# Range sums on ScalarE, merged small products and a new order list in a two-branch sequence kernel

## Chip, core and metric

The kernel runs on one core of a Trainium2 chip. The metric is the device time of one execution in microseconds (us). TensorE is called PE, VectorE DVE, ScalarE ACT, GpSimd POOL; SP is the engine that issues most DMA transfers.

## The reference

Two branches read the same x (2048 rows, 512 columns, bf16) and are mixed by a gate per row:

```python
g = _sigmoid((x * gate_w).sum(-1, keepdims=True))
a = _A_ref(x, ...)      # h[t] = Lam_bar * h[t-1] + B_bar x[t];  y = 2 Re(C h) + x * Dskip
b = _B_ref(x, ...)      # 32 heads of 16: q, k, v; features softmax(+-q w_phi), softmax(+-k w_phi)
                        # o = phi_q (phi_k^T v) / (phi_q . sum phi_k + 1e-6);  b = o @ wo
return g * a + (1 - g) * b
```

Branch a is a diagonal complex recurrence over 2048 steps with 512 states. Branch b is attention without a softmax over rows: the keys and values are first summed into a 32 x 16 matrix per head, and then every query reads that sum.

## The kernel before, in words

The fast path is one program of about 790 tasks (matmul groups, evacuations of PSUM, vector steps, DMA issues). `_fast_path` describes the tasks, and the tuple `ORDER` near the top of the file gives the sequence in which they are written out and, for each, the engine out of those that it may run on. Nothing is decided on the chip: each engine works through its own list in order, and waits in it for its operands. `pl.at(...)` and the costs in the tasks feed only the choice of buffers.

The rows of x are dealt out in four phases (f, rows 4r + f) of 512 rows. Phase 0 is loaded straight and transposed on PE (L435), in four blocks; phases 1 to 3 come by DMA transpose. Six warm-up matmuls on a zeroed tile `warm` (L425) come before, and one more after each of the first two blocks (L437). DVE writes that tile (L309). Then follow, interleaved:

- v_unit (L453): the values of 128 rows, evacuated by ACT into `vx`.
- parameters (L508 to L567): the recurrence's 512 coefficients on DVE, in tiles of 128 x 16, a complex product as four real ones.
- diagonal blocks (L583 to L589): for eight groups of states a 128 x 128 block `dgL`, the sum of the identity scaled by one column and of `swap` (the identity with halves exchanged) scaled by another. Each scaling is an instruction on ACT or DVE.
- block matrix BD (L643 to L650): w_phi without its mean, put on a block diagonal; fold (L660) multiplies it into the query and key weights.
- g_unit (L680, L685): the input of the recurrence for one group of states, carried through the four phases by a product with `dgL`. The last phase goes by DMA (L694) into a layout for the scan; scan_unit (L718 to L736) rotates, scans and rotates back on DVE; `Zs` takes the states by DMA (L748); fill_unit (L760 to L768) makes the states of the other three phases.
- k_unit (L792 to L823): keys of 256 rows, exp of plus and minus them on ACT into `E`, four sums by halves on DVE (L809) down to the softmax denominators `st1`, Ln and Exp for the reciprocal on ACT, the scaling (L816), and the sum over rows into two PSUM banks. A maximum over the denominators goes into `smax` (L812).
- q_unit (L880): the same for the queries, transposed.
- nums and smalls (L962 to L1025): numerators and denominators per head; a maximum over the query denominators goes into `qmax` (L1010).
- mix (L1027 to L1079): for each 128 rows, two scalings (L1039, one for plus and one for minus), their sum (L1041), a DMA transpose (L1056), the y products (L1048, L1052) and the product with Wo (L1065) into the same bank, the gate (L1072 or L1074), and the store (L1078).
- flag (L1101 to L1116): the gate's largest argument and the two kinds of maxima are compared with limits; if one is over, a general path runs afterwards. The flag is turned on PE, reduced, and loaded by every engine.

Of the kernel before, what the change touches and what calls it, by code (L numbers as in the profile page):

```python
# [18 lines left out]
P = 128  # L19
# [103 lines left out]
def kernel(  # L123
# [49 lines left out]
    8, 4, 6, 10, 12, 156, 14, 16, 158, 18, 22, 174, 0, 25, 176, 20, 192, 2, 162, 160, 26, 178, 196, 28, 32, 34,  # L173
    268, 30, 166, 200, 194, 36, 198, 760, 38, 276, 40, 132, 42, 164, 134, 180, 202, 44, 138, 46, 85, 73, 764, 270,
    762, 278, 77, 55, 184, 136, 272, 140, 274, 504, 168, 508, 74, 380, 506, 83, 766, 61, 182, 170, 186, 142, 79,
    208, 70, 382, 172, 81, 154, 510, 296, 298, 288, 86, 768, 144, 284, 146, 287, 212, 292, 148, 294, 96, 59, 512,
    95, 291, 56, 514, 150, 518, 211, 517, 306, 300, 67, 152, 332, 308, 302, 48, 770, 310, 304, 50, 520, 524, 523,
    65, 526, 528, 536, 338, 63, 53, 334, 446, 312, 314, 336, 342, 68, 316, 340, 772, 448, 318, 538, 322, 530, 532,
    534, 450, 344, 324, 440, 215, 444, 478, 472, 544, 320, 540, 546, 346, 326, 328, 442, 348, 330, 350, 452, 354,
    454, 456, 356, 548, 458, 474, 358, 480, 462, 460, 464, 482, 476, 216, 466, 218, 570, 98, 628, 360, 542, 384,  # L180
    100, 222, 484, 224, 362, 88, 630, 486, 226, 564, 102, 550, 104, 220, 552, 234, 602, 228, 108, 106, 488, 554,
    568, 236, 574, 566, 490, 112, 572, 230, 468, 110, 232, 494, 188, 556, 116, 248, 388, 238, 390, 250, 240, 242,
    114, 576, 190, 470, 372, 496, 252, 386, 352, 596, 578, 558, 580, 244, 606, 394, 392, 118, 254, 582, 400, 492,
    498, 586, 604, 588, 396, 600, 374, 598, 120, 694, 364, 402, 398, 500, 590, 404, 560, 608, 376, 124, 246, 406,
    256, 412, 688, 378, 408, 610, 414, 258, 612, 502, 562, 366, 122, 410, 690, 128, 692, 696, 260, 614, 416, 262,
    636, 638, 368, 632, 126, 720, 420, 698, 640, 370, 700, 422, 726, 592, 424, 618, 800, 634, 418, 616, 594, 702,
    620, 90, 642, 622, 788, 802, 728, 426, 648, 730, 722, 264, 724, 704, 644, 792, 650, 654, 646, 93, 652, 428,
    732, 790, 660, 656, 706, 734, 708, 710, 658, 662, 736, 668, 664, 670, 672, 430, 204, 812, 738, 742, 712, 206,
    280, 130, 432, 666, 818, 804, 782, 624, 776, 744, 714, 674, 794, 434, 816, 282, 814, 746, 626, 822, 820, 784,
    786, 716, 718, 748, 778, 750, 796, 780, 676, 806, 798, 810, 808, 436, 678, 758, 824, 756, 754, 752, 830, 1020,  # L190
    978, 996, 266, 984, 828, 850, 826, 854, 832, 848, 980, 852, 1302, 1314, 1022, 680, 856, 983, 986, 682, 858,
    1320, 860, 834, 998, 989, 438, 864, 684, 866, 1026, 1038, 1025, 836, 1316, 868, 1318, 1040, 1001, 862, 870,
    990, 1008, 872, 1010, 1306, 1304, 918, 842, 992, 1013, 886, 1028, 1043, 906, 882, 995, 1031, 1128, 878, 884,
    888, 912, 874, 1086, 1110, 902, 686, 1088, 876, 880, 908, 1308, 1090, 904, 898, 838, 1068, 1092, 1310, 900,
    1112, 1312, 1070, 890, 894, 930, 1130, 840, 1002, 1122, 892, 1094, 896, 1124, 846, 1072, 1004, 1014, 1044,
    1006, 914, 844, 920, 1032, 1104, 1096, 1046, 1098, 1074, 1106, 1034, 1126, 1016, 1076, 1048, 1018, 1036, 910,
    1050, 1052, 916, 1100, 1324, 1078, 1108, 924, 1200, 936, 1080, 1082, 1054, 1322, 1290, 1132, 926, 1202, 1058,
    1164, 1060, 1134, 1254, 1136, 1152, 1114, 922, 938, 928, 1138, 1204, 1116, 1158, 1154, 1062, 1166, 932, 1064,
    1084, 1066, 1188, 942, 1268, 1284, 1236, 1118, 1248, 1286, 1206, 1160, 1292, 1168, 1208, 1120, 1156, 1266,
    1190, 1182, 1176, 1184, 1288, 1232, 1102, 1193, 1210, 1162, 1270, 1256, 1170, 1194, 1186, 1178, 1230, 1294,  # L200
    1146, 1250, 1172, 1196, 1198, 1238, 1174, 1140, 948, 1234, 1276, 1056, 1142, 1148, 1272, 944, 1274, 1344,
    1180, 1150, 1144, 1212, 1214, 1252, 940, 1346, 946, 1332, 1216, 954, 1296, 1240, 1278, 1362, 1220, 1258, 1348,
    1334, 934, 1242, 1298, 1222, 1326, 1224, 950, 1380, 1226, 1364, 952, 1336, 1244, 1476, 1228, 1436, 1260, 1328,
    1368, 1366, 1434, 1452, 1440, 1280, 1370, 1262, 1438, 1356, 1382, 1350, 1442, 1372, 1392, 1454, 1352, 1478,
    1394, 1330, 956, 1338, 1358, 1354, 1396, 1458, 1386, 1416, 1340, 960, 1300, 1444, 1470, 1282, 1456, 1388,
    1374, 1418, 1360, 1376, 1472, 962, 1420, 1462, 972, 1460, 1390, 1384, 1378, 958, 1474, 1342, 974, 1398, 1426,
    1400, 1446, 1422, 1464, 1402, 966, 1480, 1448, 1424, 1406, 1265, 964, 1466, 1408, 1410, 1428, 1468, 1450,
    1412, 968, 1494, 1414, 1512, 1506, 1508, 1510, 970, 976, 1482, 1430, 1526, 1524, 1516, 1484, 1432, 1530, 1514,
    1247, 1528, 1496, 1488, 1534, 584, 1518, 1490, 740, 1492, 1542, 1544, 1546, 1532, 1520, 1548, 1498, 1536,
    1218, 1404, 774, 1487, 1500, 1523, 1552, 1550, 1538, 1502, 1554, 1566, 1557, 1505, 1560, 1541, 1568, 1570,  # L210
    1562, 1558, 1564)
# [18 lines left out]
def _fast_path(ctx, tc, A_x, A_Lambda_re, A_Lambda_im, A_B_re, A_B_im, A_C_re, A_C_im, A_log_dt, A_Dskip,  # L230
# [20 lines left out]
    warm = ctile([P, D], BF16, "warm")  # L251
# [16 lines left out]
    dgS = ctile([P, NT, P], BF16, "dgS")  # L268
# [16 lines left out]
    smax = ctile([P, NTI // 2], F32, "smax")  # L285
    qmax = ctile([P, NG], F32, "qmax")
    fl = ctile([P, 4], F32, "fl")
# [21 lines left out]
    nc.vector.memset(warm[:], 0.0)  # L309
# [42 lines left out]
    pl = _Plan({"DVE": 2.4e3, "ACT": 4.4e3, "PE": 1.1e3, "SP": 27.0e3})  # L352
# [34 lines left out]
    d_x = [pl.at(t) for t in (3.7, 4.5, 6.4, 8.4, 9.8, 11.5, 19.5)]  # L387
    d_wv0, d_wv, d_b, d_wk, d_wq, d_wo = (pl.at(t) for t in (4.5, 5.5, 17.0, 22.7, 24.8, 27.0))
    d_vec, d_wc = pl.at(9.5), pl.at(20.5)
# [5 lines left out]
    d_set = pl.at(6.2)  # L395
# [7 lines left out]
    def s_swap(e):  # L403
        for h in range(2):
            nc.vector.tensor_copy(out=swap[:, h * 64:h * 64 + 64], in_=ident[:, 64 - h * 64:128 - h * 64])
# [17 lines left out]
    def warm_fn(e):  # L423
        for _ in range(NWARM):
            MM(out=bw.t[:], lhsT=warm[:, 0:P], rhs=warm[:], start=True, stop=True)  # L425
# [4 lines left out]
    for a in range(4):  # L430
        b = pl.buf(*A1)

        def tr(e, b=b, a=a):
            for kt in range(KT):
                nc.tensor.transpose(bfv(b)[:, kt * P:(kt + 1) * P], xn[:, a, kt * P:(kt + 1) * P], ident[:])  # L435
            if a < 2:
                MM(out=bw.t[:, 0:256], lhsT=warm[:, 0:P], rhs=warm[:, 0:256], start=True, stop=True)  # L437
# [28 lines left out]
    def col():  # L466
        return sp[:, next(k_), :]
# [1269 lines left out]
```

## Time and profile before

| | us |
|---|---|
| median of 10 runs | 149.97 (149.59 to 151.3) |
| the profiled execution | 149.56 |
| its span, first to last instruction | 147.8 |
| PE busy | 140.6 |
| DVE busy | 129.4 |
| ACT busy | 115.2 |
| scalings of the mix, L1039 (32 of 128 x 512) | 12.1 |
| maxima over k sums, L812 (8 of 128 x 128) | 2.2 |
| fp32 product of 128 x 1024 on DVE, L629, each | 1.22 |

The profile holds one execution. A group of instructions is shown by its line, its engine, what it writes and reads, how often, and its busy time with the mean of one. Neighbouring instructions on one engine overlap by some 80 ns in these durations, so the distance between two starts is a little shorter than the mean duration. A wait is put down to what came last. Because durations and waits come from one execution, a sum made from them is set against that execution's own 149.56 us.

### The profile page before, as it was taken

The page shows a single profiled execution, that of the slowest core. Times are in us where ns is not written, and L with a number is a line of the kernel's source. Part 1 is how long each engine was busy: PE and PEld are TensorE (multiplying, and loading weights), DVE is VectorE, ACT ScalarE, POOL GpSimd, SP SyncE. Part 2 cuts the span into 40 slices and gives each one's busy share as a digit, 9 for nine tenths or more (in the row PEclk, how much of TensorE's full clock was granted, in tenths as well). Part 3 has the DMA queues.
Part 4 walks back from the last instruction along what each step waited for, and adds up shares of the span by engine and source line. Part 5 has one row for each costly group of instructions (what it writes and reads, how often), then busy time and mean ns, then how long its engine had stood idle before and what let it go on. Part 6 is the DMA issues. An engine that isn't in the chain of part 4 may idle for free.

```text
span 147.8 us, 3009 instructions
## 1 busy us (share of the span) xinstructions
PE 140.6 (95%) x1012; PEld 81.3 (55%) x1030; DVE 129.4 (88%) x378; ACT 115.2 (78%) x261; POOL 5.5 (4%) x15
## 2 busy tenths in 40 slices
PE   6899999999999999999999989999999999999990
PEld 2545567555665666556546545565556556445550
DVE  2328998998999999997999999999999999999610
ACT  3449899988889999889899889998787986751140
POOL 8600000000000000000000000000000000000000
PEclk9999999999999999999999999999999999999999
DMA  4999999930200031315993222143043713534712
GB/s 115 275 240 236 165 172 234 211 75 0 53 18 0 4 71 36 101 41 130 143 140 108 95 71 91 56 72 74 0 142 72 75 35 85 111 88 120 160 58 70
DMA packets 37307, 14.94 MB, mean 101 GB/s; under 512 B 29480, under 2 KB 37288, under 8 KB 37288
## 3 DMA queue, kind: packets, MB, share of 16 engines
q1 hardware_dynamic: 35824, 13.59, 44.0%
q10 hardware_dynamic: 1304, 1.12, 2.4%
q8 instruction: 9, 0.15, 0.4%
q14 instruction: 10, 0.08, 0.2%
q0 software_dynamic: 160, 0.01, 0.1%
HBM read 1.60 MB, written 2.10 MB: 25 GB/s over the span
## 4 chain that ended last, share of the span: by engine, by line
PE 83%; DVE 7%; DMA 5%; issue 1%; ACT 1%; SPq 0%; DVEq 0%
PE pp L680 19%; PE pp L1048 17%; PE pp L792 9%; PE pp L453 9%; PE pp L1065 8%; PE pp L962 5%; PE pp L685 4%; PE pp L880 3%; DMA late<-late 2%; DMA c<-c 2%; PE pp L1052 2%; PE pp L425 2%; PE pp L823 2%; DVE c L728 2%; PE pp L660 1%
## 5 line engine op out<-in xcount | busy, mean ns | idle before, releaser
L680 PE MATMUL pp<-xT,BT 128*128 128x512 bf16 x123 | 31.5, 381 | 0.2
L1048 PE MATMUL pp<-CT,Gs 128*128 128x512 bf16 (+1 forms) x99 | 23.5, 362 | 0.2
L680 PEld LDWEIGHTS <-BT 128*128 128x128 bf16 x128 | 17.8, 145 | 8.8
L1072 ACT ACTIVATE late<-pp,Gg 128x512 bf16<-128x512 f32 (+1 forms) x16 | 10.8, 673 | 11.1 <-PE pp L1065 10.9
L243 ACT ACTIVATE ET<-pp 128x512 bf16<-128x512 f32 x32 | 17.7, 612 | 1.0 <-PE pp L880 1.0
L243 ACT ACTIVATE E<-pp 128x512 bf16<-128x512 f32 x32 | 17.7, 607 | 0.2 <-PE pp L792 0.2
L1065 PE MATMUL pp<-Wo,late 128*128 128x512 bf16 (+1 forms) x67 | 16.1, 367 | 0.2 <-DMA late<-late 0.2
L453 PE MATMUL pp<-Wv,xT 128*128 128x512 bf16 x61 | 15.6, 386 | 0.6 <-ACT xT L381 0.5
L792 PE MATMUL pp<-Wk,xT 128*128 128x512 bf16 x64 | 15.6, 380 | 0.0
L880 PE MATMUL pp<-xT,Wq 128*128 128x512 bf16 x61 | 15.1, 379 | 0.5 <-DVE elate L978 0.3
L1048 PEld LDWEIGHTS <-Gs 128*128 128x128 bf16 x104 | 9.7, 98 | 7.9
L381 ACT CAST Gs<-pp 128x512 bf16<-128x512 f32 x20 | 11.7, 593 | 2.3 <-PE pp L685 2.3
L962 PE MATMUL pp<-KS,ET 128*128 128x144 bf16 (+1 forms) x128 | 12.0, 225 | 0.1
L970 ACT CAST late<-pp 128x384 bf16<-128x384 f32 (+1 forms) x24 | 10.3, 455 | 2.0 <-PE pp L962 2.0
L962 PEld LDWEIGHTS <-ET 128*128 128x128 bf16 x128 | 9.2, 98 | 4.3 <-issue 0.8
L970 ACT CAST elate<-pp 128x512 bf16<-128x512 f32 (+2 forms) x20 | 9.6, 513 | 2.0 <-PE pp L962 1.9
L816 DVE TENSOR_TENSOR E<-E,rc 128x2048 bf16<-128x2048 bf16 x8 | 9.7, 1218 | 0.5 <-ACT rc L243 0.5
L792 PEld LDWEIGHTS <-xT 128*128 128x128 bf16 x64 | 6.1, 98 | 6.9
L381 ACT CAST vx<-pp 128x512 bf16<-128x512 f32 x16 | 9.0, 588 | 0.7 <-PE pp L453 0.7
L453 PEld LDWEIGHTS <-xT 128*128 128x128 bf16 x64 | 5.8, 98 | 6.5 <-ACT xT L381 0.8
L880 PEld LDWEIGHTS <-Wq 128*128 128x128 bf16 x64 | 5.9, 97 | 6.3 <-issue 0.4
L728 DVE TENSOR_TENSOR_SCAN c<-sp,c 128x512 bf16<-128x512 f32 x8 | 9.3, 1208 | 0.0
(180 smaller groups left out, 252.4 us busy)
## 6 DMA issues: line engine op xcount, KB each, us to landing
Zs<-c SPq DMA_DIRECT2D x32, 64.0 KB, 2.1
out_dram<-late SPq DMA_DIRECT2D x9, 128.0 KB, 1.9
c<-c SPq DMA_DIRECT2D x16, 64.0 KB, 2.0
CT<-ET SPq DMA_DIRECT2D x8, 128.0 KB, 5.6
out_dram<-late ACTq DMA_DIRECT2D x6, 128.0 KB, 2.2
Wo<-in_B_wo_dram SPq DMA_DIRECT2D x4, 128.0 KB, 3.0
xn<-in_A_x_dram SPq DMA_DIRECT2D x2, 128.0 KB, 3.4
Wv<-in_B_wqkv_dram ACTq DMA_DIRECT2D x1, 256.0 KB, 3.4
```

What stands on the lines that cost most here:

```text
L243: return nc.scalar.activation(**kw)
L381: nc.scalar.copy(out=o, in_=view(b))
L453: MM(out=f32v(b), lhsT=xT[:, kt, tcols(f, a)], rhs=Wv[:, kt, :], start=(kt == 0), stop=(kt == KT - 1))
L680: MM(out=f32v(b), lhsT=BT[:, kt].rearrange("p r (q t) -> p (r q) t", t=NT)[:, :, j + 4 * h], rhs=xT[:, kt, f * NCH:(f + 1) * NCH], start=( ...
L728: nc.vector.tensor_tensor_scan(out=bw_.t[:, ri], data0=rb, data1=b1.t[:, ri], initial=0.0, op0=ALU.mult, op1=ALU.add)
L792: MM(out=f32v(b), lhsT=xT[:, kt, tcols(f, a)], rhs=Wk2[:, kt, :], start=(kt == 0), stop=(kt == KT - 1))
L880: MM(out=f32v(b), lhsT=Wq2[:, kt, g * P:(g + 1) * P], rhs=xT[:, kt, f * NCH:(f + 1) * NCH], start=(kt == 0), stop=(kt == KT - 1))
L962: MM(out=f32v(b)[:, i * w:(i + 1) * w], lhsT=ets[f].t[:, q // HG, q % HG, cs], rhs=KS[:, q // HG, q % HG, 0:w], start=True, stop=True)
L970: nc.scalar.copy(out=o2.t.rearrange("p a b -> p (a b)")[:, q0 * P:(q0 + n) * P].rearrange("p (q c) -> p q c", c=P), in_=blk()[:, :, 0:P])
L1048: MM(out=f32v(py)[:, 0:w], lhsT=st, rhs=CT[:, tt // 2 + 4 * (tt % 2), n * w:n * w + w], start=(tt == 0), stop=False)
L1065: MM(out=f32v(py)[:, 0:w], lhsT=oT.t[:, g, :], rhs=Wo[:, g, hs], start=False, stop=(g == HG - 1))
L1072: nc.scalar.mul(out=ot.t[:, hs], in_=f32v(py)[:, 0:w], mul=Gg[:, ti:ti + 1])
```

## The change

- The warm-up matmuls read a constant tile of ones that every program sets up at its start on POOL. The memset on DVE is gone. After the first block of x there is one more warm-up matmul, of 512 columns.
- The four diagonal blocks of a half are one DVE product: a pattern with ones on both diagonals (`swap` now holds the identity plus its exchanged halves), times a table `dgW` of fp32 weights that is set by four small copies. The separate scalings are gone.
- The parameter products are made two at a time on tiles of 128 x 32 (`p5`, `p6`).
- BD is made with one masked product for all four blocks, after a fused subtraction of the mean.
- The k denominators of all pairs are kept in one tile `Sk`. In place of the maxima, ACT sums them along the row with its accumulator, once over all 1024 (k) and once per phase over 256 (q), into columns of `fl`. Each sum is compared with the limit; the flag is the smallest of the comparisons.
- The two scalings of a tile in the mix are one instruction over 1024 elements.
- `ORDER` is a new list, with new costs and due times.

```diff
-    warm = ctile([P, D], BF16, "warm")
+    warm = nc.const_aps.tensor(1.0, [P, D], BF16)
...
-    nc.vector.memset(warm[:], 0.0)
...
-            nc.vector.tensor_copy(out=swap[:, h * 64:h * 64 + 64], in_=ident[:, 64 - h * 64:128 - h * 64])
+            VT(out=swap[:, h * 64:h * 64 + 64], in0=ident[:, 64 - h * 64:128 - h * 64], in1=ident[:, h * 64:h * 64 + 64], op=ALU.add)
...
-            if a < 2:
-                MM(out=bw.t[:, 0:256], lhsT=warm[:, 0:P], rhs=warm[:, 0:256], start=True, stop=True)
+            for w in ((512, 256), (256,), (), ())[a]:
+                MM(out=bw.t[:, 0:w], lhsT=warm[:, 0:P], rhs=warm[:, 0:w], start=True, stop=True)
...
-            VT(out=t2, in0=pwr[n - 1], in1=lr_, op=ALU.mult)
-            VT(out=t3, in0=pwi[n - 1], in1=li_, op=ALU.mult)
-            VT(out=t4, in0=pwr[n - 1], in1=li_, op=ALU.mult)
-            VT(out=t5, in0=pwi[n - 1], in1=lr_, op=ALU.mult)
+            VT(out=tX, in0=pw[n - 1], in1=two(lr_), op=ALU.mult)
+            VT(out=tY, in0=pw[n - 1], in1=two(li_), op=ALU.mult)
...
+    def w_dl(e):
+        for v, hs in ((lr_, ((0, 0), (64, 1))), (ns1, ((0, 1), (64, 0)))):
+            for p0, half in hs:
+                nc.vector.tensor_copy(out=dgW[p0:p0 + 64, :, half].rearrange("p (j h) -> p j h", h=2),
+                                      in_=v[p0:p0 + 64, 8:16].rearrange("p (h j) -> p j h", h=2))
+    t_wdl = pl.add({"DVE": 330.0}, w_dl, deps=[tp4], rank=6)
...
-            parts.append(pl.add({"ACT": 330.0, "DVE": 165.0}, scaled(dgL[:, tt, :], ident[:], lr_[:, ucol(tt)]), deps=[tp3], rank=6 - jj))
-            parts.append(pl.add({"ACT": 330.0, "DVE": 165.0}, scaled(dgS[:, tt, :], swap[:], ns1[:, ucol(tt)]), deps=[tp4, t_swap], rank=6 - jj))
...
+            VT(out=dgL[:, s_].rearrange("p t (h c) -> p t h c", h=2), in0=swap[:].rearrange("p (h c) -> p h c", h=2).unsqueeze(1).to_broadcast([P, 4, 2, 64]),
+               in1=dgW[:, s_].unsqueeze(3).to_broadcast([P, 4, 2, 64]), op=ALU.mult)
...
-        t_sx.append(pl.add(_dve(128), lambda e: nc.vector.tensor_reduce(
-            out=smax[:, pair:pair + 1], in_=b1.t[:].rearrange("p a b c -> p (a b c)"), axis=AX.X, op=ALU.max), deps=prev, bufs=[b1], rank=-3))
...
+    dump = iot[:].bitcast(BF16)
+    t_fk = pl.add({"ACT": 1060.0}, lambda e: aact(out=dump, in_=Sk[:].rearrange("p a b c -> p (a b c)"), func=ACT.Copy, accum_out=fl[:, 1:2]),
+                  deps=t_sx + t_tab)
...
-        t_qm.append(pl.add(_dve(256), lambda e: nc.vector.tensor_reduce(out=qmax[:, f:f + 1], in_=smv()[:, :, 0, :], axis=AX.XY, op=ALU.max),
-                           deps=[x3], bufs=[b], rank=r_))
+        t_qm.append(pl.add({"ACT": 430.0}, lambda e: aact(out=dump[:, 0:256].rearrange("p (a b) -> p a b", b=8), in_=smv()[:, :, 0, :], func=ACT.Copy,
+                                                          accum_out=fl[:, 2 + f:3 + f]), deps=[x2, t_fk], bufs=[b], rank=r_))
...
-        for sgn in range(2):
-            def sc(e, sgn=sgn):
-                v = o2.t[:, sgn].rearrange("p (g d h) -> p g d h", g=HG, d=Dh)
-                VT(out=v, in0=v, in1=als[f].t[:, a, sgn * H:(sgn + 1) * H].rearrange("p (g h) -> p g h", g=HG).unsqueeze(2).to_broadcast([P, HG, Dh, 8]), op=ALU.mult)
+        def sc(e):
+            v = o2.t.rearrange("p s (g d h) -> p (s g) d h", g=HG, d=Dh)
+            VT(out=v, in0=v, in1=als[f].t[:, a].rearrange("p (g h) -> p g h", h=8).unsqueeze(2).to_broadcast([P, 2 * HG, Dh, 8]), op=ALU.mult)
```

In the instruction lists that result, PE has the same matmuls plus the one of 512 columns, DVE 337 compute instructions in place of 379, and ACT 259 in place of 270 (DMA issues counted). DVE takes over from ACT two evacuations of G, one of x, two final ones and six small copies. The order of the loads at the start is unchanged. On PE the second block's transposes and warm-up now come before the first V product. The ACT sum over k stands between the last two evacuations of G. Among the last Wo products no two stand next to each other, as one pair did before.

## The prediction

> **What bounds the kernel now.** I read four views: the busy line of the page, the table of stretches, the chain of work that ended last, and the waits. First the busy line and four of the ten-microsecond stretches.
>
> ```profile
> PE 140.6 (95%) x1012; PEld 81.3 (55%) x1030; DVE 129.4 (88%) x378; ACT 115.2 (78%) x261; POOL 5.5 (4%) x15
> ```
>
> ```profile
> 0.00:10.00 10.00, 8.26 (x47) 3.84 (x47) 2.85 (x22) 4.12 (x6) 5.46 (x15) 1.00 0.84 208
> ...
> 50.00:60.00 10.00, 9.89 (x69) 6.16 (x69) 10.00 (x21) 9.51 (x20) 0.00 (x0) 1.00 0.19 48
> ...
> 80.00:90.00 10.00, 9.48 (x112) 5.81 (x111) 9.93 (x31) 8.77 (x21) 0.00 (x0) 1.00 0.26 85
> ...
> 140.00:147.80 7.80, 3.73 (x28) 2.26 (x26) 0.90 (x3) 1.85 (x3) 0.00 (x0) 1.00 0.26 71
> ```
>
> In a stretch the first two numbers after its length are PE and PEld, then DVE and ACT. A busy PE need not be a PE at its peak, so I checked it: the chain shows four 128x512 matmuls in 0.86 us again and again, 0.216 us each. Costing the whole instruction list at the pace of the chain (512 columns 0.216, 144 columns 0.062, 128 columns 0.056, 68 columns 0.032, one column 0.024) gives 138.3 us. The first pieces run at half that pace (0.457 us for 512 columns), which adds 2.3. The sum, 140.6, is the busy time: **PE is the bound, and it streams without gaps almost throughout.** DVE is as full (10.00 of 10 in six stretches) but PE hardly ever waits for it. What can be won is PE's idle time, 147.8 - 140.6 = 7.2 us: 1.74 in the first stretch, 0.5 spread over 10 to 80, 0.52 in 80 to 90, 0.35 in 90 to 140, and 4.07 in the last. Of the last, 3.88 lies behind PE's last matmul (143.92): the flag's way through DVE, its load and the branch. The change leaves that part as it is.
>
> The two ends of the chain and PE's named waits:
>
> ```profile
> 0.95 0.28 DVE warm L309
> 1.28 2.74 PE pp L425 x6
> 4.02 0.44 PE pp L435 x4
> 4.48 0.59 ACT xT L381
> 5.12 0.93 PE pp L453 x2
> 6.05 0.23 PE pp L435 x4
> ...
> 136.89 0.32 PE pp L1065 x2
> 137.21 3.51 DMA late<-late
> 140.76 1.04 PE pp L1065 x4
> ```
>
> ```profile
> PE pp L425 <- DVE warm L309: 1.3, 1, 1.3
> ...
> PE pp L453 <- ACT xT L381: 0.5, 1, 0.5
> ...
> PE pp L880 <- DVE elate L978: 0.3, 1, 0.3
> ...
> PE pp L1065 <- DMA late<-late: 0.2, 1, 0.2
> ```
>
> So PE begins at 1.28 because DVE's memset of the warm-up tile comes first; it stands idle 0.46 us before the first V product, for ACT's copy of the first transposed block; it waits 0.3 us for a DVE copy that frees a PSUM bank; and near the end about 0.35 us for a DMA transpose (four matmuls from 139.55 end at 140.41, the next starts at 140.76). The chain's 3.51 us of DMA there is not idle PE: other products run under it.
>
> **The change, part by part.** *Constant warm-up.* The memset (0.27 us) and PE's wait for it go. Nothing else of the kernel holds PE's first matmul; ACT and DVE begin at 0.83 and 0.95, so PE should begin near 0.95: 0.33 earlier. One 512-column dummy is added (0.457 at the slow pace), the second block's transposes and its dummy move ahead of the first V product, and the copy that this product waits for goes to DVE (425 ns for the same tile instead of 585). New start: six dummies 0.95 to 3.69 (the first x block was there at 3.54), transposes to 4.13, dummies to 4.82, transposes to 5.26, dummy to 5.49, then two V products, then two that need ACT's copy of the second block (0.2 + 0.585 after 5.26, so 6.05). The wait of 0.46 is filled, with dummy work in part. When the pace doubles decides the rest. In the trace the slow pace ends between 5.12 and 6.05. Counted from PE's first matmul that is up to 4.7 us, so 5.65 in the new kernel, and two V products end near 5.97, the next two follow at 6.05, and the point where 16 transposes and the first four V products are done moves from 7.26 to 6.95: -0.3. The Trainium skill (TensorE: Matmul & The Clock Gate, "What's actually happening") speaks against that: the activity window is free-running and does not begin with the kernel. If the pace then changes at the same 6.05 on the span's clock, the point is at 7.1: -0.16. The same rule allows a change as early as some 3.4 us after the start, an estimate from that page, which gives about -0.5, since the third V product then waits for the copy. The granted clock reads 1.00 in every row, so only the pace shows this. I take **-0.25**, ends -0.1 and -0.5. Next in line are the loads: the first half of x for the next block landed at 7.9 (issued 2.64, 5.3 to landing) and is needed at 8.6, B at 16.1 (10.84 and 5.3), needed at 17.9. Close, but none late.
>
> *DVE work removed.* Spacing of like instructions in the timeline, not their mean, is the price. Eight maxima over k sums (mean 280 ns, spacing near 200): -1.6. Four over q sums (two in 0.74 us, so 0.33 each): -1.3. Parameter products: 29 instructions took 3.23 us, 0.11 each; nine fewer: -1.0. Scaling: two of 418 ns took 0.75 us, so 0.67 for a pair; one of 1024 elements has a spacing of 0.60: 16 times 0.07 is -1.1. Block matrices: 13 scalings at 0.165 and two sums at 0.34 make 2.8 (and three ACT scalings of 0.42); the new way is four small copies (0.5) and two products of 128x512 with fp32 weights. bf16 rows of that size show 418 ns; the skill's page VectorE: DVE Perf Modes ("The perf-mode tier table") says that a tensor_tensor with fp32 input runs at single rate, and the fp32 row (1220 ns for 1024) gives 0.61 to 0.69 at half the size. By the bf16 row the part saves 1.5 us, by the rule 1.0; I take 1.0. BD in three instructions instead of seven: -0.4. Together about -6.4 us of DVE. The new list gives DVE work of ACT's: two more 512-column evacuations of G, one of x, two final ones and six small copies, about +3.7. DVE ends near 126.
>
> *What moves to ACT.* One sum over 1024 elements (nearest row: the table sine of that size, 1060 ns) and four over 256 (418): +2.7. Away go three diagonal scalings, the five evacuations and the small copies: -5.6. ACT ends near 112, with 2 to 3 us idle in each ten after 110. The accumulator's own price is shown by no row: between nothing and, if it needs a separate read of the size of the smallest ACT rows, 0.2 us each, +1.0 in all; I take nothing.
>
> None of this is on the path while PE streams: 9 us of savings on engines that PE doesn't wait for are worth nothing by themselves. They are worth what PE waits for late operands.
>
> *The new order.* PE gets the same matmuls plus one dummy (0.22 at full pace, under the wait). What it can take back is 0.52 in 80 to 90, 0.35 in 90 to 140, 0.35 at the DMA and perhaps 0.1 in 10 to 80. DVE is about 2 us ahead by 80 us (smax, parameters, blocks and BD lie before it), so the PSUM copy and the K-V blocks that set the waits there come sooner: -0.35 (ends 0 and -0.7). At the end the last Wo products are each separated by a group of other products in the new list, where before two stood together, so the DMA transpose has cover: -0.3 (ends 0 and -0.4). Rest: -0.1 (ends +0.3 and -0.2).
>
> **Sum.** -0.25 - 0.35 - 0.3 - 0.1 = -1.0 us. The profiled execution took 149.56 (span 147.8 and 1.76 around it), so about 148.6. The median of the ten runs is 149.97, 0.4 above it, since four of the ten lie near 150.9; the same step from the median gives **149.0**.
>
> **Rivals.** *PE bound, nothing returned but the start.* Against my sum speaks that PE's waits from 10 to 140 are many and tiny (0.05 us per stretch), which look like hand-over times that no order removes, and that a new order makes its own small waits. Then only -0.1 to -0.4 is left, and the median is 149.7. *ACT stands in the way: slower.* The 1.06 us sum over k sits in ACT's list between the two last evacuations of G for the last scan, and waits for the last k sum from DVE. Behind it wait that evacuation, its exchange by DMA (3.44 us in the chain), the scan and the second half of the y products. Those products come about 1.2 us earlier in the new list (94.5 against 95.7), and the last Z copies, estimated from the end of issue at 93.05, land near 94.6. If DVE's k sum is late, the delay is 1.06 plus that lateness; it decides once the delay is over the 1 us or so that DVE is now ahead. A delay of 2.5 us would leave PE idle for about 1.5 past the cover: 149.97 - 0.25 + 1.5 = 151.2. For it: DVE was at 10.00 of 10 there. Against it: its lead. *A large return:* the pace doubles early (-0.5) and nearly all inner waits go (-1.3): 148.2. *Not doing what it says:* the constant operand could hold PE's first matmul as long as the memset did; -0.25 becomes 0, 149.2.
>
> **How the numbers follow.** About 0.5% (0.75 us) is what a measurement of this kernel can tell from no change, so faster means below 149.2. My forecast with its own range 148.6 to 149.4: 0.50. Large return: 0.12. Start alone, or a warm-up that starts no sooner: 0.27. ACT in the way: 0.11. The likeliest gives 149.0. Down to 148.1 and up to 150.1 no more than two in ten are left out: the lower end takes the early doubling with the middle of the rest, the upper end the mild form of the ACT delay. Faster: 0.5 x 0.85 + 0.12 + 0.05 of the start alone = 0.60. Slower by over 0.75: 0.09. Same: 0.31.
>
> **What would show it.** First warm-up matmul near 0.95 and no gap before the first V product; the half-pace pieces ending by 6.0; the first B product near 17.9 to 18.1, not 18.44; the stretch 80 to 90 at 9.8 or more for PE; no PE wait for a DMA transpose near the end; PE's last matmul near 142.9 and 3.9 us behind it as before. DVE near 126 and ACT near 112 busy would confirm the costs. I am wrong if PE shows new waits for ACT or the Z copies from 85 to 100, or if PE's idle time between first and last matmul stays near 2.0 us.

## The result and the profile after

| | before | after | ratio, 95% interval |
|---|---|---|---|
| median of the runs taken together with the change | 150.59 us (51 runs) | 149.42 us (14 runs) | 0.9935 [0.9914, 0.9956] |
| the same, second series | 150.19 us (42 runs) | 149.55 us (7 runs) | 0.9939 [0.9916, 0.9961] |

The change takes 0.6% off, about 0.95 us, which is the step that the prediction made from its median (149.97 to 149.0, a ratio of 0.9935). The medians of the kernel before differ from series to series (149.94 to 150.59), so only ratios within a series are compared below. A ratio is the estimate on record and not the quotient of the two medians, which is 0.9922 in the first series and 0.9957 in the second; steps of 0.2% are not to be read from either.

The two profiles that are shown side by side do not show that gain: the profiled execution of the changed kernel took 150.02 us (span 148.1), one of the slowest of its runs, and that of the kernel before 149.56, one of its fastest. This has to be kept in mind while reading them. The busy line and five stretches of the profile after:

```profile
PE 141.4 (95%) x1013; PEld 81.5 (55%) x1031; DVE 127.9 (86%) x336; ACT 112.8 (76%) x257; POOL 5.3 (4%) x15
```

```profile
0.00:10.00 10.00, 8.40 (x40) 3.59 (x41) 2.89 (x18) 3.80 (x6) 5.27 (x15) 1.00 0.92 179
50.00:60.00 10.00, 9.95 (x60) 6.17 (x60) 10.00 (x19) 9.55 (x20) 0.00 (x0) 1.00 0.18 46
80.00:90.00 10.00, 9.89 (x122) 6.25 (x122) 9.86 (x26) 9.89 (x24) 0.00 (x0) 1.00 0.29 94
90.00:100.00 10.00, 9.61 (x84) 6.04 (x85) 9.97 (x32) 9.46 (x23) 0.00 (x0) 1.00 0.46 87
140.00:148.10 8.10, 4.34 (x38) 3.17 (x36) 1.45 (x7) 1.16 (x2) 0.00 (x0) 1.00 0.25 69
```

PE is still the bound, DVE and ACT have become a little lighter. The stretch 80 to 90 went from 9.48 to 9.89 for PE; ACT went from 8.77 to 9.89 there. The next stretch takes most of that back: it fell to 9.61 from the 9.95 of the profile before,

```profile
90.00:100.00 10.00, 9.95 (x86) 6.11 (x86) 10.00 (x34) 9.49 (x21) 0.00 (x0) 1.00 0.29 71
```

since PE's waits that were at 83.7 and 88.6 now stand at 90.3 and 91.7. The last stretch has more PE work because everything is later in this execution. Why, the waits of PE and pieces of the chain tell:

```profile
PE pp L421 <- PEq L1715: 0.9, 1, 0.9
PE pp L449 <- DMA xT<-in_A_x_dram: 0.5, 1, 0.5
PE pp L875 <- DVE elate L975: 0.2, 1, 0.2
PE pp L959 <- ACT iot L241: 0.2, 1, 0.2
```

```profile
2.64 6.69 DMA xT<-in_A_x_dram
9.38 1.90 PE pp L449 x8
...
19.00 2.59 PE pp L676 x12
...
143.32 0.87 PE pp L1060 x8
```

PE begins at 0.93 now, the wait for the memset is gone and so is the one for ACT's copy before the first V product. In their place stands a wait of 0.54 us at 9.38 for the first rows that come by DMA transpose: they landed 6.7 us after their issue, where the profile of before had 5.3 for the same issue in the same list. So the first B product (L676) came at 19.00, not at 18.44. At the other end the wait for the DMA transpose before the last Wo products is gone. L959 waits for ACT's `iot`, which is where the new q sum dumps its elements.

Two things are needed to read PE's idle time. A product of 512 columns is shown with 0.38 us though the next one starts 0.216 after it, so an idle time that the profile shows is about 0.16 us less than what the stop costs from start to start: the 0.19 us at the end of the profile before cost 0.35. And the two profiles hold 1012 and 1013 products where PE loaded weights for 18 more; in the eight profiles that hold 1030 or 1031 products most of the idle gaps of 0.05 us are absent. In each of the two profiles gaps of that size, 18 and 20 of them, make up 1.0 us of PE's idle time. The starts around such a gap are 0.43 us apart, the time of two products, so they look like products without a record rather than waits.

### The profile page after: what moved, and what is told of

It is laid out like the page before. It is cut to its first block, busy times and chain, and to the rows that moved or that the text cites. A ratio compares the mean times of both kernels' runs of the same rounds, so it can differ in the third digit from the quotient of the medians.

```text
span 148.1 us, 2969 instructions
## 1 busy us (share of the span) xinstructions
PE 141.4 (95%) x1013; PEld 81.5 (55%) x1031; DVE 127.9 (86%) x336; ACT 112.8 (76%) x257; POOL 5.3 (4%) x15
## 4 chain that ended last, share of the span: by engine, by line
PE 78%; ACT 7%; DMA 6%; SPq 5%; issue 1%; DVE 0%
PE pp L1043 19%; PE pp L676 18%; PE pp L1060 9%; PE pp L787 9%; PE pp L449 7%; DMA xT<-in_A_x_dram 5%; PE pp L959 4%; PE pp L681 3%; SPq L743 3%; PE pp L1047 2%; ACT ET L241 2%; ACT late L967 2%; PE pp L875 2%; PE pp L818 2%; DMA Zs<-c 1%
## 5 line engine op out<-in xcount | busy, mean ns | idle before, releaser
L676 PE MATMUL pp<-xT,BT 128*128 128x512 bf16 x125 | 31.7, 381 | 0.2
L676 PEld LDWEIGHTS <-BT 128*128 128x128 bf16 x128 | 17.9, 145 | 8.9 <-issue 0.3
L241 ACT ACTIVATE ET<-pp 128x512 bf16<-128x512 f32 x32 | 18.2, 618 | 0.6 <-PE pp L875 0.5
L1067 ACT ACTIVATE late<-pp,Gg 128x512 bf16<-128x512 f32 (+1 forms) x14 | 9.4, 675 | 10.8 <-PE pp L1060 10.8
L241 ACT ACTIVATE E<-pp 128x512 bf16<-128x512 f32 x32 | 17.1, 602 | 0.4 <-PE pp L787 0.3
L959 PE MATMUL pp<-KS,ET 128*128 128x144 bf16 (+1 forms) x128 | 12.4, 225 | 0.2 <-ACT iot L241 0.2
L377 ACT CAST Gs<-pp 128x512 bf16<-128x512 f32 x18 | 10.4, 593 | 2.3 <-PE pp L676 1.8
L959 PEld LDWEIGHTS <-ET 128*128 128x128 bf16 x128 | 9.3, 98 | 4.8 <-issue 0.5
L967 ACT CAST elate<-pp 128x384 bf16<-128x384 f32 (+2 forms) x21 | 9.6, 499 | 2.2 <-PE pp L959 2.2
L967 ACT CAST late<-pp 128x384 bf16<-128x384 f32 (+2 forms) x23 | 10.0, 486 | 1.3 <-PE pp L959 1.1
```

The costliest lines, as they stand in the source:

```text
L241: return nc.scalar.activation(**kw)
L377: nc.scalar.copy(out=o, in_=view(b))
L676: MM(out=f32v(b), lhsT=BT[:, kt].rearrange("p r (q t) -> p (r q) t", t=NT)[:, :, j + 4 * h], rhs=xT[:, kt, f * NCH:(f + 1) * NCH], start=( ...
L959: MM(out=f32v(b)[:, i * w:(i + 1) * w], lhsT=ets[f].t[:, q // HG, q % HG, cs], rhs=KS[:, q // HG, q % HG, 0:w], start=True, stop=True)
L967: nc.scalar.copy(out=o2.t.rearrange("p a b -> p (a b)")[:, q0 * P:(q0 + n) * P].rearrange("p (q c) -> p q c", c=P), in_=blk()[:, :, 0:P])
L1067: nc.scalar.mul(out=ot.t[:, hs], in_=f32v(py)[:, 0:w], mul=Gg[:, ti:ti + 1])
```

## The experiments

All ratios are to the kernel before, in the same series. To compare profiles whose starts differ I use four marks of each one: the time at which PE's clock was granted in full (the start of the trace's first clock record), the start of the first B product (the chain puts it some 0.16 later, since neighbours overlap), the distance from there to the end of PE's last matmul, and what lies behind that.

| kernel | ratio, 95% interval | profiled us | full clock from | first B at | to PE's last | behind it |
| --- | --- | --- | --- | --- | --- | --- |
| before, first profile |  | 149.56 | 5.81 | 18.27 | 125.65 | 3.85 |
| before, again | 1.0012 [0.9992, 1.0032] | 149.34 | 4.48 | 18.16 | 125.43 | 3.85 |
| old list, constant | 0.9977 [0.9961, 0.9992] | 150.25 | 3.69 | 19.01 | 125.59 | 3.85 |
| old list, light DVE | 0.9987 [0.9962, 1.0012] | 150.00 | 5.15 | 18.08 | 126.18 | 3.85 |
| old list, all else | 1.0025 [1.0008, 1.0043] | 149.84 | 3.56 | 17.93 | 126.27 | 3.85 |
| after | 0.9935 [0.9914, 0.9956] | 150.02 | 5.22 | 18.84 | 125.50 | 3.78 |
| after, again | 0.9939 [0.9916, 0.9961] | 149.64 | 3.80 | 17.94 | 126.13 | 3.78 |
| new list, memset | 0.9955 [0.9931, 0.9980] | 149.51 | 6.13 | 18.31 | 125.52 | 3.79 |
| new list, one dummy | 0.9934 [0.9911, 0.9957] | 149.83 | 6.67 | 18.61 | 125.54 | 3.78 |
| new list, heavy DVE | 1.0452 [1.0412, 1.0492] | 157.96 | 6.55 | 18.48 | 133.81 | 3.78 |
| new list, sums on DVE | 1.0032 [1.0016, 1.0048] | 150.39 | 4.77 | 17.91 | 126.91 | 3.78 |
| k sum late | 0.9953 [0.9936, 0.9970] | 149.04 | 4.11 | 17.95 | 125.52 | 3.78 |
| k sum late, q sum early | 0.9958 [0.9940, 0.9977] | 148.91 | 3.77 | 17.81 | 125.53 | 3.78 |
| the same, x loaded by ACT | 1.0088 [1.0055, 1.0120] | 150.46 | 5.16 | 19.38 | 125.51 | 3.78 |

My theory at the outset: the lighter engines alone are worth nothing, and the gain is in the start and in the list's cover of waits. The rivals: the relief of VectorE is the gain; and the loads, not the warm-up, decide the start.

### Both kernels once more

No edit. For the kernel before:

> The kernel before, unchanged, profiled once more. If the landing of the first loads varies from execution to execution by a microsecond (theory: load variation), this profile has other landing times than the first one (x, second group of rows: 5.3 us from issue to landing there) and the first B product moves with them, 18.4 to 19.0; the ratio is 1.000 within 0.3%. If the landings are a property of the list (rival), they are 5.3 us again and the first B product stands at 18.44 within 0.05.

For the changed kernel:

> The changed kernel, unchanged, profiled once more. Load variation: the xT rows land 5.3 to 6.7 us after their issue, and when they land at the short end PE doesn't wait at 9.4 and the first B product comes at 18.1 to 18.4 instead of 19.00, the span near 147.2. List (rival): the 0.54 us wait at 9.4 is there again with the same landing times, and the span is 148.1 within 0.1. Ratio to before 0.992 to 0.995 by both.

**Measured.** The repeat of the kernel before is at 1.0012, so differences of 0.2% are within the noise. Its xT loads landed in much the same time (median 5.3 us from issue, 5.1 in the first profile) and the first B product came 0.1 us from where it was; for this kernel the two executions don't show the variation. The changed kernel does: median landing 5.4 instead of 6.1, no wait at 9.4, the first B product at 17.94, 0.9 us earlier than in its first profile. But its span fell by only 0.3, to 147.85 and not to the 147.2 that was expected. Of the 0.9 us, 0.6 was lost again on the way to PE's last matmul (126.13 against 125.50), in a wait that the first profile had not:

```profile
PE pp L959 <- ACT ET L241: 0.4, 1, 0.4
```

It stands at 83.9, and ACT is named for it, but the last thing that PE's queue waits for there is DVE: it passes that wait at 83.81, 0.04 after DVE's last K-V block. DVE's timeline of the same execution shows where it comes from. The bracket is the idle time ahead of an instruction and what ended it:

```profile
69.79 0.69 DVE L713 TENSOR_TENSOR c<-c,Tcs 128x1024 bf16<-128x1024 bf16 x1 [0.52 <-DMA c<-c]
...
83.62 0.16 DVE L860 TENSOR_TENSOR KS<-pp,mask 64x16 bf16<-64x16 f32 x1
```

DVE waited 0.52 us for the exchange of a scan by DMA, had no idle time after it to catch up (10.00 of 10 in 70 to 80), and finished the last K-V block `KS` at 83.78. PE asks for it 65.4 us after its first B product, so at 83.35, and had to wait. In all the other profiles of the new list with DVE's light work and the sums on ACT, DVE had no idle time at that exchange, and PE's first KS product came 65.4 us after the first B product.

**What follows.** In this execution PE came early and then waited for DVE at about 83.8. An earlier start is worth its full size only in an execution in which DVE and the exchange keep up, as they did in the profiles of the two kernels with a late k sum (first B product at 17.95 and 17.81, no wait there). One execution of each does not tell how often that is so.

### The constant warm-up, alone and left out

```
-    warm = ctile([P, D], BF16, "warm")
+    warm = nc.const_aps.tensor(1.0, [P, D], BF16)
-    nc.vector.memset(warm[:], 0.0)
```

Done alone in the kernel before:

> The kernel before with the warm-up products on the constant and without the memset, its own list and all its VectorE work. If the constant warm-up is what the change gains by (theory: start), the first product is near 0.93, the transposes, which wait for the x rows at 4.7, are not sooner, the clock steps earlier by about 0.35 us, and the ratio is 0.997 to 0.998 (0.25 to 0.4 us less). If the loads gate the start (rival), the first product is near 0.93 too, but the first B product stays at 18.4 to 19.0 as the landings have it and the ratio is 0.999 to 1.000.

Undone in the changed kernel:

> The changed kernel with the warm-up products on a tile that VectorE sets to zero, as in the kernel before. Start theory: the first product is back at 1.28, the clock steps 0.35 us later, and the ratio to before is 0.996 to 0.997 (the change loses 0.3 to 0.4 us of its gain). Loads gate the start: the wait for xT at 9.4 shrinks by what the start lost, and the ratio is 0.993 to 0.994, that of the changed kernel.

**Measured.** Alone 0.9977, so 0.35 us, with an interval from 0.1 to 0.6. Left out 0.9955, between the ranges of the two theories: 0.27 us less than the change by the ratios of 0.9935 and 0.9939, but the intervals overlap, and in the same series the medians stand the other way (149.47 and 149.55). The first matmul is at 0.93 and 1.28 as expected. So the constant's gain is shown in the old list; in the new list its size is not told from nothing. The load rival is right for single executions: the profile of the constant alone shows PE waiting 0.52 us for the rows of xT at 9.25, and its first B product at 19.01. The ratio of the runs shows that the gain is not lost to this on average; how often it happens, no trace tells.

### The second dummy

```
-            for w in ((512, 256), (256,), (), ())[a]:
+            for w in ((256,), (256,), (), ())[a]:
```

> The changed kernel without the second dummy product (512 columns) behind the first transposes, so that TensorE pauses for about 0.4 us near 4.3 while it waits for the second x tile. If unbroken work ends the half pace (start theory): the doubling of the pace moves from 5.7 to 6.1 to 9, and the ratio rises by 0.001 to 0.003 over that of the changed kernel, to 0.995 to 0.997. If pauses of this length don't matter (rival): the doubling stays at 5.7, and the ratio is 0.993 to 0.994.

**Measured.** 0.9934, nothing lost, although PE now pauses 0.56 us at 4.4. When the pace doubled can be read from the time that like matmuls take. First the dummies of the kernel with both sums moved (512 and 256 columns, 0.64 at the slow pace without the overlap, 0.32 at the full one), then single V products of the kernel with the heavy DVE and of that with one dummy:

```profile
3.84 0.49 PE L431 MATMUL pp<-const-bfloat16-1.0 128*128 128x512 bf16 x2
```

```profile
5.87 0.63 PE L451 MATMUL pp<-Wv,xT 128*128 128x512 bf16 x1
```

```profile
5.57 0.63 PE L449 MATMUL pp<-Wv,xT 128*128 128x512 bf16 x1
...
6.00 0.63 PE L449 MATMUL pp<-Wv,xT 128*128 128x512 bf16 x1
```

All three kernels begin at 0.93. In the first the pace has doubled by 3.9: at the full pace a product of 512 columns shows 0.38, and the two dummies together 0.49. In the other two a V product still takes 0.63 and they follow each other after 0.43. The clock records agree with the pace: they begin, at 1.00, at 3.77, 6.55 and 6.67 in these three. (Before its first record the trace says nothing of the clock, and the column of the stretches counts such time as full; that is why it reads 1.00 from the start.) The kernel with the pause is the latest of all, by 0.12 us. That lies in the range of the start theory (6.1 to 9), while the ratio is that of the rival; since the kernel with the heavy DVE was nearly as late without a pause, this one execution decides nothing about the pause.

**What follows.** The moment lies between 3.56 and 6.67 in the ten executions whose PE starts at 0.93, so the time since the first matmul does not fix it. Where it lies at 4.8 or before and no late load stops PE, the first B product is at 17.81 to 17.95 whatever the moment; at 6.55 and 6.67 it is at 18.48 and 18.61. The dummy adds nothing that shows in the runs.

### VectorE's relief without the list, and the list without the relief

The lighter work in the order of before. The tasks of the maxima are left empty and so the range check is left out:

```
-            out=smax[:, pair:pair + 1], in_=b1.t[:]..., axis=AX.X, op=ALU.max), deps=prev, bufs=[b1], rank=-3))
+        t_sx.append(pl.add(_dve(128), lambda e: None, deps=prev, bufs=[b1], rank=-3))
...
+                if sgn:
+                    return
+                v = o2.t.rearrange("p s (g d h) -> p (s g) d h", g=HG, d=Dh)
```

> The kernel before with its own order list and its memset, but with VectorE's work as the change has it: block matrices by one masked product, paired parameter products, one scaling per tile; the maxima are gone and no sums stand for them, so that it leaves out the range check. ScalarE loses its share of the block matrices. Theory of the list: PE waits for neither engine, so lighter engines under the old order give 0.998 to 1.000; the gain of the change sits in its list and its start. Rival, relief: VectorE is the second engine that limits the stretch from 40 to 130, and 0.993 to 0.996 of the time comes back without the new list, PE's 80 to 90 stretch going from 9.48 to 9.8 or more.

The heavy work in the new order:

```
+            for tt in range(4 * jj, 4 * jj + 4):
+                VS(out=dgL[:, tt, :], in0=ident[:], scalar1=lr_[:, ucol(tt)], scalar2=None, op0=ALU.mult)
+                VS(out=dgS[:, tt, :], in0=swap[:], scalar1=ns1[:, ucol(tt)], scalar2=None, op0=ALU.mult)
+            VT(out=dgL[:, s_], in0=dgL[:, s_], in1=dgS[:, s_], op=ALU.add)
...
+            nc.vector.tensor_reduce(out=qmax[:, f:f + 1], in_=smv()[:, :, 0, :], axis=AX.XY, op=ALU.max)
...
+            for sgn in range(2):
```

> The changed kernel, its list, constant warm-up and ScalarE sums kept, with VectorE's removed work put back in the same places of the list: two scalings and an addition per block matrix, one product per masked block, nine small dummy products for the unpaired ones, the maxima beside the sums, two scalings per output tile. VectorE's busy time goes from 128 to 134 us or more. Theory of the list: VectorE's spare time covers most of it and the ratio is 0.993 to 0.997. Rival, relief: the list was made for light tasks, PE gains waits for VectorE in 40 to 130 of 1 us or more in all, and the ratio is 1.000 to 1.010.

**Measured.** Relief alone: 0.9987, not told from nothing, with DVE at 124.9 us busy instead of 129.4. The theory holds, and the trace shows where the relief went. In the light kernel's DVE timeline:

```profile
66.23 1.23 DVE L822 TENSOR_TENSOR E<-E,rc 128x2048 bf16<-128x2048 bf16 x1 [0.48 <-ACT rc L243]
...
78.96 0.69 DVE L725 TENSOR_TENSOR c<-c,Tcs 128x1024 bf16<-128x1024 bf16 x1 [1.12 <-DMA c<-c]
```

DVE reaches the last scan's exchange 1.1 us before it has landed and waits. The exchange hangs on PE's products, so DVE can't run ahead of it in this list; the K-V blocks stand behind it and end at 83.70, no earlier than before (83.51, 83.42).

The list with heavy work fails badly: 1.0452, DVE 135.7 us busy, 6.3 more than in the kernel before. My theory had said 0.993 to 0.997, the rival 1.000 to 1.010; both are wrong here. PE's waits in that kernel (0.9 for its start left out):

```profile
PE pp L688 <- DVE Gs L381: 2.1, 1, 2.1
PE pp L1073 <- DMA late<-elate: 1.2, 1, 1.2
...
PE pp L968 <- DVE KS L869: 0.8, 1, 0.8
PE pp L663 <- DVE Gs L381: 0.5, 1, 0.5
PE pp L884 <- DVE elate L984: 0.5, 1, 0.5
```

These make 5.1 of the 8.3 us by which the way from the first B product to PE's last matmul is longer than in the changed kernel, and some 0.16 more each, counted from start to start. Most of the rest is PE's clock, which no other profile shows lowered between its first clock record and PE's last product:

```profile
39.19 0.38 PE L688 MATMUL pp<-Gs,dgL 128*128 128x512 bf16 x1 [2.06 <-DVE Gs L381]
```

```profile
40.70:44.00 3.30, 3.30 (x22) 1.78 (x23) 3.13 (x9) 2.86 (x8) 0.00 (x0) 0.50 0.19 42
```

The third number from the right is the granted clock. The clock records have 0.50 from 40.68 to 44.09, after PE had stood still for 2.06 us until 39.19; the products of that time are 0.43 apart, and 3.4 us at half pace cost an estimated 1.7. So this wait cost more than its own length. The kernel is harsher than an undoing: all block scalings are on DVE, in one piece in front of other work (some ran on ACT before), the maxima stand beside the sums, and the dummies stand where the paired products are. It shows that this list cannot carry 8 us more of DVE's work; what an exact undoing would cost is not shown. **What follows.** Relief and list are not two gains that add. DVE has little slack in this list, and most of what was taken from it was used up by the evacuations that it took over from ACT.

### The sums on VectorE

```
-    t_fk = pl.add({"ACT": 1060.0}, lambda e: aact(out=dump, in_=Sk[:]..., func=ACT.Copy, accum_out=fl[:, 1:2]),
+    t_fk = pl.add({"DVE": 1060.0}, lambda e: nc.vector.tensor_reduce(out=fl[:, 1:2], in_=Sk[:]..., axis=AX.X, op=ALU.add),
```

and the four q sums likewise.

> The changed kernel with the five sums of the range check as reductions on VectorE, at the same places of the list. ScalarE loses about 3.6 us (sums and accumulator reads), VectorE gains about 2.3 us. Theory that the sums stand in the way on ScalarE: the 0.16 us wait of PE near 91.5 behind a sum goes, ScalarE's 80 to 90 stretch falls from 9.9 to below 9.3, and the ratio to before is 0.990 to 0.993. Rival, the sums cost nothing where they are: 0.993 to 0.996. If VectorE is the tighter engine from 80 to 130, its 1.3 us sum there delays scans and the ratio is 0.996 to 1.001.

**Measured.** 1.0032, above the ranges of all three theories; the third, DVE as the tighter engine, had the direction. The sums at the same places on DVE cost 0.95% more than on ACT, 1.4 us, for 2.4 us of DVE work. Two waits of PE carry it:

```profile
PE pp L959 <- DVE KS L860: 0.8, 1, 0.8
PE pp L959 <- DVE fl L1007: 0.6, 1, 0.6
```

ACT was not the engine in the way. From 70 to 95 work added to DVE comes back as PE's waits, and in this list the sums' place on ACT is worth more than the start.

### The change without its list

The old order with the light DVE, the constant and the ACT sums (the k sum at about 115 us, two q sums moved to where ACT has room). The edit is that of the light kernel with the sums of the change put in the place of the empty tasks.

> The kernel before with its own order list, and with all else that the change does: the lighter VectorE work, the constant warm-up, the sums on ScalarE (the k sum put at about 115 us, the last two q sums at 117 and 131, where ScalarE has room; the tasks of the maxima left empty). If the parts add up (constant alone 0.9977, VectorE relief alone 0.9987), the ratio is 0.9964, and the list is worth the remaining 0.25% to the 0.9937 of the change. If the relief pays only together with the earlier start (rival), it is 0.993 to 0.995 and the list is worth nothing. If the sums hurt where a list was not made for them: 0.998 to 1.001.

**Measured.** 1.0025, the outcome named for sums in a list that was not made for them. The first B product is early (17.93), and 0.7 us more than in the kernel before goes by until PE's last matmul. PE's waits there:

```profile
PE pp L881 <- DVE elate L981: 0.3, 1, 0.3
PE pp L965 <- DVE KS L866: 0.3, 1, 0.3
PE pp L965 <- ACT iot L241: 0.2, 1, 0.2
PE pp L1070 <- DMA late<-late: 0.2, 1, 0.2
```

The first is in the kernel before too. The second is the early start given back at 83.55: DVE waited 0.96 us for the same exchange. The third is a q sum that holds a PSUM bank, the fourth the DMA transpose at the end. **What follows.** With nearly all else equal (the dummy of 512 columns is left out, and the list also deals out engines: ACT is busy 116.6 us here and 112.8 in the changed kernel), the list is worth 0.9%, from 1.0025 to 0.9935; a part of it, the 0.24 us at the first q sum, is owed to the place that the old list has for it. It is the list that lets the other parts count: DVE waits for a scan's exchange in all five profiles of the old list (up to 1.12 us at a time) and in one of nine of the new one (0.52), and the last Wo products cover for the DMA transpose.

### Moving the sums, and a load

The k sum (728) moved in `ORDER` behind 1160, from 73 us to 115; then the first q sum (816) behind 820 as well; then, on top, one load moved to ACT's queue.

```
-    174, 728, 622,
+    174, 622,
...
-    nc.sync.dma_start(out=xn[:, 2:4], in_=x0[:, 2:4])
+    nc.scalar.dma_start(out=xn[:, 2:4], in_=x0[:, 2:4])
```

> The changed kernel with the k sum moved in the list from about 73 us, where it stands in front of the evacuation that the last scan's exchange waits for, to about 115, where ScalarE has room; nothing else moves. Theory that the sum delays the exchange: c is evacuated 0.5 to 1.1 us sooner near 74, the wait for ScalarE near 84 (0 to 0.4 us, by the exchange's landing) and those at 90 and 91.5 go or shrink, ratio 0.990 to 0.9925. Rival, the scan has slack there: PE's 80 to 100 stretch keeps its 0.3 us of waits and the ratio stays at 0.993 to 0.995.

> As the kernel with the late k sum, and the first q sum stands 1.4 us earlier on ScalarE, right behind the logarithm of the denominators, so that its PSUM buffer comes free before PE asks for it near 91. If that buffer is the wait of 0.16 us: it goes, 0.1% less than with the late k sum alone. Rival: the sum now delays the evacuation of Q products behind it, PE waits 0.2 to 0.5 us near 90 instead, and the ratio is the same or 0.1 to 0.2% more.

> As the kernel with the two sums moved, and the load of the last two x tiles is issued by ScalarE behind its half of Wv instead of by SP: these tiles are asked for at 1.3 instead of 2.13, and SP's first DMA transpose at 2.1 instead of 2.64. If the issue times gate the start (load theory): no wait for x at 4.5 to 6.5 nor at 9.4, the first B product at 17.3 to 17.8, and a ratio 0.2 to 0.4% below that of the kernel with the two sums moved. If the transfers share the DMA engines' bandwidth (rival): the rows land when they did, or the weights land later, and the ratio is the same within 0.15%, or up to 0.2% more.

**Measured.** 0.9953 and 0.9958, neither told from the change (0.9935, 0.9939) nor better by ratio (0.990 to 0.9925 had been expected of the first if the sum were in the way), although their medians (149.22 and 149.10) and profiled executions (149.04 and 148.91) are the lowest of all; the series' median of before was low too, 149.94. So the candidate for the fastest version stays undecided. What the trace does show is the mechanism. ACT in the changed kernel, and then with the sum moved:

```profile
73.20 0.58 ACT L377 CAST c<-pp 128x512 bf16<-128x512 f32 x1 [0.19 <-PE pp L681]
73.68 1.06 ACT L241 ACTIVATE iot<-Sk 128x1024 bf16<-128x1024 f32 x1
74.64 0.19 ACT L241 ACTIVATION_READ_ACCUMULATOR iot<-Sk 128x1 f32 x1
74.73 0.58 ACT L377 CAST c<-pp 128x512 bf16<-128x512 f32 x1
```

```profile
72.32 0.59 ACT L375 CAST c<-pp 128x512 bf16<-128x512 f32 x1 [0.19 <-PE pp L679]
73.40 0.59 ACT L375 CAST c<-pp 128x512 bf16<-128x512 f32 x1 [0.49 <-PE pp L679]
```

The distance of the two evacuations falls from 1.53 to 1.08, so the sum delays the exchange by 0.45 us, and DVE comes to that exchange without a wait all the same. With the q sum moved, one wait of 0.27 us for DVE's copy, at 90.9, stands in place of the two of 0.16 at 89.4 and 90.8. No net gain either.

Loading x by ACT made it 1.3% slower, which none of my numbers allowed for. ACT's timeline:

```profile
6.38 0.25 ACTq L320 DMA_DIRECT2D vec_n<-in_A_Lambda_im_dram  x1
6.67 0.59 ACT L375 COPY xT<-pp 128x512 bf16<-128x512 bf16 x1 [4.56 <-DMA Wv<-in_B_wqkv_dram]
```

The issue of the last small load at 6.38 waits on a semaphore, and the trace tells which: number 104, the one that SP's half of Wv raises, whose last part landed at 6.35. The loads of SP and ACT use eight semaphores over again; with one more load among ACT's, this issue got another number. With the load on SP it waits on 102, that of the first x block, and runs at 3.41. ACT's copy of the x block stands behind that issue, and PE waits 1.45 us for the copy. So the cost comes from which earlier load an issue has to wait for, not from the size of what is in ACT's queue: ACT's own large loads had landed by 5.45. The test does not tell whether issue times or bandwidth gate the loads, since this wait got in the way.

## Why the prediction was right, point by point

**The total** was right: -1.0 us and 0.9935 predicted, 0.9935 and 0.9939 measured. That it fits so closely is in part luck, for only some of the steps under it are found in the traces, and two of the signs that the prediction had named as proof against it did turn up in the profile after: PE's idle time between its first and last matmul is 1.97 us (2.18 in the repeat), and at 91.7 there is a new wait for ACT. Of the 1.97, 0.54 is the late load, and 1.0 are the gaps of 0.05 that look like missing records; the 2.00 of the profile before holds as much of them. So half of what this sign counts, and nearly all of the 0.45 us that the prediction named as returnable from 10 to 80 and from 90 to 140, seem to be no waits.

- **Start, -0.25 (ends -0.1 and -0.5): right.** First matmul at 0.93 for 0.95; the gap before the first V product gone; worth 0.35 us alone, and not told from nothing in the changed kernel. *"Close, but none late"* on the loads failed in single executions (0.54 us at 9.38). The full clock came between 3.56 and 6.67; the alternative that I weighed against it, a window that does not begin with the kernel (the Trainium skill, TensorE: Matmul & The Clock Gate, "What's actually happening"), agrees with that better than a count from PE's first matmul, by which these executions should have been alike. The estimate of some 3.4 us for the earliest change fits the 3.56 only when it is counted from the start of the span; from PE's first product it is 2.6. A large gain from an early change did not show: with the full clock from 3.56 or from 4.77 the first B product stood at the same place (17.93 and 17.91).
- **"9 us of savings on engines that PE doesn't wait for are worth nothing by themselves": right** in its direct form (old list, light DVE: 0.9987). It hid something: DVE and PE arrive at the K-V blocks together. In the profiles of before PE's first product follows DVE's last block after 0.15 us (83.51 and 83.66), as it does wherever PE waited for it, and in the profile after it is 0.2. So DVE work that is added or kept there is dear at once (sums on DVE, +1.4 us).
- **80 to 90, -0.35: not shown.** PE's share did reach 9.89, but the next stretch lost nearly as much, and the distance from the first B product to PE's last matmul is the same in the two profiles of before (125.65, 125.43) and in most of the new list (125.50 to 125.54). The wait for the PSUM copy (0.31 at 88.6) became two waits of 0.16, one of them the wait for a q sum which I had priced at nothing on PE's path.
- **End, -0.3: right at its place, but taken back elsewhere.** The wait for a DMA transpose before the last Wo products shows in three of five profiles of the old list (0.19, 0.34, 0.18 idle, so 0.35, 0.50, 0.34 from start to start) and in none of the new list with light DVE. Over five profiles that is 0.24 us. Since the distance to PE's last matmul is no shorter, other waits take it back, those at 90.3 and 91.7 among them. The tail behind that matmul, which the prediction left as it was, went from 3.85 to 3.78; the cause is not known.
- **ACT in the way: right in mechanism, not decisive.** The k sum does delay the exchange, by 0.45 us and not by 1.06 plus lateness, since without the sum ACT waits 0.49 us for PE at that place; and the exchange had that much to spare.
- **Sizes.** DVE 127.9 for 126 (the prediction's own terms give 126.7): the relief measured 4.5 us (light kernel) where I had summed 6.4. ACT 112.8 for 112: the accumulator is read by an instruction of its own, 0.19 to 0.27 us for each of the five sums, the upper end that I had set aside. The product with fp32 weights took 688 ns per 512 columns, the price by the rule and not that of the bf16 row (418).

**What stays open.** The start (0.35 where it was tested alone) and the tail (0.07) explain about 0.4 of 0.95 us. The rest shows in timed runs only. It would fit that in slower executions of the kernel before PE waits for the exchange at 83.5, as it does for 0.47 and 0.31 us in the two other kernels with the old list whose start is early. But both profiles of the kernel before are among its fastest runs, and the idle time there is 0.08 and 0.11. So this is argued, not shown.

## What to carry to other kernels

Before pricing relief at nothing or at its full size, compare when the second engine and the bound reach the point at which they meet: here they met within 0.1 us, so taking work away gained nothing, while adding 2.4 us cost 1.4. A hand-made order list is made for the durations of its tasks; test an edit with the list that goes with it, and don't add up parts that were measured under different lists. A total that fits is no proof of the terms: look for each of them at its place, and then for what took it back. With a start that hangs on loads, take a second profile of each kernel before reading a difference of half a microsecond from a pair.

## What the runs showed of the hardware

- A ScalarE sum comes with a separate read of the accumulator, 0.19 to 0.27 us each.
- The clock was granted in full between 3.56 and 6.67 us in ten executions whose PE starts alike at 0.93. Until then a product of 512 columns takes 0.43 from start to start, and 0.216 after it.
- After PE had stood still for 2.06 us, its clock was granted at 0.50 for 3.4 us, beginning 1.5 us after the end of the wait (heavy DVE, one execution).
- The same DMA transpose at the start of the kernel landed 5.3 us after its issue in one execution and 6.7 in another.
